# Windowed attention feeding a normalised MLP: score and value steps in pairs from one PSUM pool

## The chip, the cores and the metric

The kernel runs on one core of a Trainium2 chip. The metric is device time in microseconds (us); before the change the median of three runs is 309.67 us (309.27 to 309.78). The core's engines are TensorE (PE in the profile, with its weight loads as PEld), VectorE (DVE), ScalarE (ACT), GpSimd (POOL) and SyncE (SP, which here issues most DMAs). Each works through its own list of instructions in order and waits on semaphores for the others.

## The reference

Attention with a causal window of 64 positions, for 8 batches of 8 heads, 576 positions and a head width of 64. Its output, with the heads side by side, is the input of a normalised two-layer MLP with a residual:

```python
scores = scale * np.matmul(q, k.transpose(0, 1, 3, 2))          # scale = 1/8
mask = (rel >= 0) & (rel < 64)                                   # rel = query - key
attn = softmax(np.where(mask, scores, -1e9)); y = np.matmul(attn, v)
x = y.transpose(0, 2, 1, 3).reshape(8, 576, 512)
xn = (x - mean) / np.sqrt(var + 1e-06) * g_ln
out = x + np.maximum(xn @ w_ch1, 0.0) @ w_ch2                    # 512 -> 2048 -> 512
```

## The kernel before

**Groups.** The work is cut into nine groups. Groups 0 to 7 are the first 512 positions of the eight batches, four blocks of 128 queries each. Group 8 collects the last 64 positions of all batches; its blocks are called tails, and block i of it belongs to batches 2i and 2i+1.

**Attention of one block** has two parts on TensorE.

- A score step (`s_mm`): 16 matmuls, each 64 rows deep (one head's width), write 64 queries against 128 keys. Even heads go to one 2 KB PSUM tile and odd heads to another, both from the pool `ps_s`, which has two buffers. Two exponentials on ScalarE (L294), one a tile, write the probabilities `pt` in fp16, and `s_mask` (L301) multiplies them by the window's mask on VectorE.
- A value step (`b_step`): 16 matmuls (L321), each 64 columns wide, write the 128 by 8 by 65 values, with the row sums as the 65th column, into one 4 KB PSUM tile `xps` from the pool `ps_x`, which has one buffer. VectorE takes the reciprocal of the sums (L324), scales into `x_norm` (L327) and computes mean and variance (L329, L332).

From group 2 on `z_step` then makes the normalised row `z` on GpSimd in four instructions (L351 to L354), and `zt_step` transposes it into `zT` (by DMA, or for two blocks by TensorE).

**MLP of one group.** From group 2 on it has 30 units, numbered from 0. Units 0 to 15 are `l1`: four matmuls with 512 columns each (L401) into a tile of `ps_mm`, which has two buffers, and a ReLU out of it on ScalarE into `hrT` (L405). So unit i+2 can't begin before the ReLU of unit i has read its tile. Units 16 to 29 are `stage`: the second layer as seven half-size products, two units each, in the order 1, 2, 6, 5, 7, 4, 3. `product` (L478) sums into the PSUM banks A, B and C; product 6 goes on in bank A on top of product 1. `post` (L485) adds a bank to `x_norm` on VectorE, and product 6 can't begin before the `post` of product 1 has read bank A. Products 6, 5, 7 and 3 take sums of `hrT` that VectorE makes in `s_sums` (L452): for the first eight units in slots 8 to 11, for the next four in slots 13 and 14, for the last four in slots 15, 15, 19 and 21.

**The order is written by hand.** Each engine executes in the order in which the loop at the end issues. While group g runs its MLP, the attention of group b = g+1 is issued between its units, and the loads, casts and transposes of group n = g+2: `at(i, f, ...)` puts a call behind unit i, in slot i, and calls in one slot come in the order of the `at` lines. Before the change the steps of group b stand so:

```python
at((2, 7, 12)[j - 1], s_mm, b, j)          # j = 1, 2, 3; block 0 in slot 27 of the group before
at((3, 8, 13)[j - 1], s_mask, b, j)
at((2, 7, 12, 17)[j], b_step, b, j)
at((2, 7, 12, 17)[j], z_step, b, j)
```

Four casts of q and k to fp16 (L128) on GpSimd, two for each, stand in slots 11 (three) and 16 (one); the k casts are transposed by TensorE (`t_main`, L229), the q casts by DMA from SP's queue in slot 13. Group 1 has other units, with the same scheme. The last group's first layer uses half-size products too (L592), in tiles that it takes from all pools.

Of the kernel before, what the change touches and what calls it, by code (L numbers as in the profile page):

```python
# [20 lines left out]
def kernel(  # L21
# [34 lines left out]
    ps_s = ctx.enter_context(tc.tile_pool(name="pss", bufs=2, space=PSUM))  # L56
    ps_x = ctx.enter_context(tc.tile_pool(name="psx", bufs=1, space=PSUM))
# [9 lines left out]
    mhalf = p_const.tile([128, 1], FP32, tag="mhalf", name="mhalf")  # L67
# [192 lines left out]
    def s_mm(g, j, pe_mask=False):  # L260
        sc = [ps_s.tile([128, NHP, 2, 64], FP32, tag="sc", name=f"sc_{g}_{j}_{par}") for par in range(2)]
        pt = p_pt.tile([128, 2, NHP, 2, 64], FP16, tag="pt", name=f"pt_{g}_{j}")
        pts[(g, j)] = pt
        if pe_mask:
            m = mbias[:, :]
            mb = bass.AP(tensor=m.tensor, offset=m.offset, ap=[m.ap[0], [0, NHP * 2], m.ap[1]])
            for par in range(2):
                nc.tensor.matmul(
                    out=sc[par][:, :].rearrange("p h w i -> p (h w) i"), lhsT=ident16, rhs=mb,
                    start=True, stop=False, skip_group_check=True,  # L270
                )
        for hp in range(NHP):
            for iw in range(2):
                for par in range(2):
# [11 lines left out]
                    nc.tensor.matmul(out=sc[par][:, hp, iw, :], lhsT=lhsT, rhs=rhs,  # L286
                                     start=not pe_mask, stop=True, skip_group_check=pe_mask)

        for par in range(2):
            o, i = pt[:, par], sc[par][:, :]  # L290
            if XQ <= g < NGRP - 1:
                o = o.rearrange("p h w (r j) -> p (h w) r j", j=4)
                i = i.rearrange("p h w (j r) -> p (h w) r j", j=4)
            nc.scalar.activation(out=o, in_=i, func=AF.Exp, bias=0.0, scale=scale)  # L294
# [8 lines left out]
    def b_step(g, kb):  # L303
        kblk = f"{g}_{kb}"
        sfx, nb = ("r", 2) if g == NGRP - 1 else ("", None)
        if kb % 2 == 0:
            if (g, kb // 2) not in x_norm:
                for h in ((1, 0) if g // 2 == 2 else (0, 1)):
                    x_norm[(g, h)] = p_xn.tile([128, 2, DM], FP32, tag="xn" + sfx, name=f"xn_{g}_{h}", bufs=nb)
        xv = x_norm[(g, kb // 2)][:, kb % 2, :]  # L310
        xn = xv.rearrange("p (h d) -> p h d", h=H)
        xps = ps_x.tile([128, H, 128], FP32, tag="xps", name=f"xps_{kblk}")
        pt = pts.pop((g, kb))
        for h in range(H):
            par, hp = h % 2, h // 2
            for r in range(2):
                if sfx:
                    rhs = vT[kb][:, r, h, :]
                else:
                    rhs = (vA if r else vB)[g][:, kb, h, :]  # L320
                nc.tensor.matmul(out=xps[64 * r:64 * r + 64, h, :D + 1], lhsT=pt[:, par, hp, r, :], rhs=rhs,  # L321
                                 start=True, stop=True)
        rcp = p_blk.tile([128, H], FP32, tag="rcp", name=f"rcp_{kblk}")
        nc.vector.reciprocal(out=rcp, in_=xps[:, :, D])  # L324
        rcp_b = bass.AP(tensor=rcp.tensor, offset=rcp[:, :].offset,
                        ap=[rcp[:, :].ap[0], rcp[:, :].ap[1], [0, D]])
        nc.vector.tensor_tensor(out=xn, in0=xps[:, :, 0:D], in1=rcp_b, op=ALU.mult)  # L327
        stats = p_blk.tile([128, nc.vector.BN_STATS_DIM], FP32, tag="stats", name=f"stats_{kblk}")
        nc.vector.bn_stats(out=stats, in_=xv)  # L329
        if g not in mvg:  # L330
            mvg[g] = p_grp.tile([128, 4, 2], FP32, tag="mvg" + sfx, name=f"mvg_{g}", bufs=1 if sfx else 2)
        nc.vector.bn_aggr(out=mvg[g][:, kb, :], in_=stats)  # L332
        if g < 2 and (g, kb) != (0, 2):
            z_step(g, kb)

    def z_step(g, kb):
# [15 lines left out]
        nc.gpsimd.tensor_tensor(out=rs, in0=ve, in1=mhalf, op=ALU.pow)  # L352
# [39 lines left out]
    def mlp_units(g, split=0, three=False, seven=True):  # L392
# [173 lines left out]
        def l1_product(n, d):  # L566
# [11 lines left out]
            }[n]  # L578
            if n == 1:
                pool, tag = (ps_mm, "mm") if d == 2 else (ps_s, "sc")  # L580
# [451 lines left out]
```

## Time and profile before

| | |
|---|---|
| median of three runs | 309.67 us |
| the profiled execution, first to last instruction | 305.9 us |
| PE busy | 295.4 us (97%), 3061 matmuls |
| DVE busy | 220.6 us (72%), 412 instructions |
| POOL busy | 173.3 us (57%), 256 instructions |
| ACT busy | 150.7 us (49%), 253 instructions |
| PE's longest wait on another engine | 2.3 us, once, at the start |
| granted TensorE clock, mean | 0.995 |

The profile's span runs from the first to the last instruction of one execution; the 3.8 us up to the median lie around it. Idle time of an engine that is not the bottleneck costs nothing, so what counts is what holds PE up. In a timeline the columns are the start, the duration, the engine, the line, the operation, output and inputs, their shape and the count; a bracket at the end gives idle time ahead of the instruction and what ended it. Ends of matmuls are modelled, so PE is best read by its starts.

### The profile page before, as it was taken

How to read it: one execution, taken by the hardware profiler on the slowest of the kernel's cores; microseconds unless marked ns; L12 is line 12 of the kernel's file. 1: busy time of each engine (PE TensorE's matmuls, PEld its weight loads, DVE VectorE, ACT ScalarE, POOL GpSimd, SP SyncE). 2: the span in 40 equal slices, each digit the busy share in tenths (PEclk: the TensorE clock that was granted, in tenths of full speed). 3: DMA queues.
4: the chain of work that ended last, by engine and by line, in shares of the span. 5: the costliest groups of instructions: out<-in, count | busy, mean ns of one | idle time of the engine just before them, and what ended most of it. 6: DMA issues, size and time to landing. Idle time of an engine off the chain costs nothing.

```text
span 305.9 us, 7582 instructions
## 1 busy us (share of the span) xinstructions
PE 295.4 (97%) x3061; PEld 196.4 (64%) x3061; DVE 220.6 (72%) x412; ACT 150.7 (49%) x253; POOL 173.3 (57%) x256
## 2 busy tenths in 40 slices
PE   6989999999999999999999999999999999999992
PEld 4557545687454478547854786469646854788882
DVE  0778696767766995589656965896669685789972
ACT  2586635587227733775157527752475046306500
POOL 7589676564952789179806983698146507014300
PEclk9999999999999999999999999999999999999998
DMA  8999999999776997899189997993790399003014
GB/s 191 266 385 301 314 366 286 303 284 236 150 181 228 243 172 147 280 280 127 35 243 303 204 160 245 298 155 70 215 175 19 53 189 208 19 17 139 0 38 103
DMA packets 113669, 58.35 MB, mean 191 GB/s; under 512 B 83617, under 2 KB 104609, under 8 KB 113634
## 3 DMA queue, kind: packets, MB, share of 16 engines
q1 hardware_dynamic: 112576, 54.67, 74.0%
q0 software_dynamic: 768, 2.80, 3.8%
q8 instruction: 24, 0.39, 0.5%
q10 hardware_dynamic: 290, 0.40, 0.5%
q14 instruction: 11, 0.09, 0.1%
HBM read 38.80 MB, written 9.44 MB: 158 GB/s over the span
## 4 chain that ended last, share of the span: by engine, by line
PE 89%; SPq 4%; DMA 2%; POOL 1%; ACT 1%; DVE 1%; issue 0%; ACTq 0%
PE hps L401 30%; PE pA L478 12%; PE pB L478 8%; PE pC L478 8%; PE hph L537 6%; PE ch L413 6%; PE xps L321 4%; PE sc L286 4%; PE ch L554 3%; PE tp L229 3%; PE lA L592 2%; DMA w1s<-in_moe_w_ch_dram 2%; SPq L141 2%; POOL w1g L190 1%; SPq L89 1%; PE lC L592 1%
## 5 line engine op out<-in xcount | busy, mean ns | idle before, releaser
L401 PE MATMUL hps<-zT,w1g 128*128 128x512 f16 x416 | 95.3, 380 | 0.0
L405 ACT ACTIVATE hrT<-hps 128x512 f16<-128x512 f32 x104 | 62.3, 599 | 39.3 <-PE hps L401 35.7
L401 PEld LDWEIGHTS <-w1g 128*128 128x128 f16 x416 | 38.6, 98 | 43.3 <-issue 0.7
L294 ACT ACTIVATE pt<-sc 128x512 f16<-128x512 f32 x72 | 39.0, 594 | 27.7 <-PE sc L286 20.5
L478 PEld LDWEIGHTS <-sS 128*128 128x128 f16 x448 | 43.4, 98 | 4.9
L351 POOL TENSOR_SCALAR rsz<-mvg 128x1 f32<-128x1 f32 x28 | 10.2, 364 | 60.6 <-DVE mvg L332 59.8
L128 POOL CAST qk<-qk 128x1024 f16<-128x1024 f32 x32 | 36.3, 1147 | 11.3 <-DMA qk<-in_k_dram 5.6
L478 PEld LDWEIGHTS <-hrT 128*128 128x128 f16 x336 | 32.4, 98 | 5.5 <-ACT hrT L637 0.3
L301 DVE TENSOR_TENSOR pt<-pt,mask 128x1024 f16<-128x1024 f16 x32 | 27.5, 867 | 8.4 <-ACT pt L294 8.4
L215 ACT COPY qkT<-tp 128x1024 f16<-128x1024 f16 x16 | 16.1, 1012 | 34.1 <-PE tp L229 34.1
L485 DVE TENSOR_TENSOR xn<-pA,xn 128x512 f32<-128x512 f32 x28 | 19.2, 685 | 16.7 <-PE pA L478 11.1
L478 PE MATMUL pC<-w2s,sS 128*128 128x256 f16 x224 | 27.1, 273 | 0.0
L478 PE MATMUL pA<-wT,sS 128*128 128x256 f16 x224 | 26.9, 273 | 0.0
L354 POOL TENSOR_SCALAR z<-xn,rsz 128x512 f16<-128x512 f32 x28 | 24.9, 888 | 2.9
L327 DVE TENSOR_TENSOR xn<-xps,rcp 128x512 f32<-128x512 f32 x36 | 24.9, 691 | 1.5 <-DMA out_dram<-xn 0.3
L329 DVE BATCH_NORM_STATS2 stats<-xn 128x6 f32<-128x512 f32 x36 | 25.0, 695 | 1.2
L324 DVE RECIPROCAL rcp<-xps 128x8 f32<-128x8 f32 x36 | 7.3, 204 | 24.7 <-PE xps L321 24.7
L452 DVE TENSOR_TENSOR sS<-hrT 128x512 f16<-128x512 f16 (+1 forms) x40 | 24.5, 613 | 0.6 <-ACT hrT L405 0.6
L537 PE MATMUL hph<-zT,w1g 128*128 128x256 f16 x192 | 23.8, 273 | 1.0 <-DVE zT L371 0.5
L321 PEld LDWEIGHTS <-pt 128*64 128x64 f16 x576 | 12.2, 110 | 13.7 <-issue 5.5
L352 POOL TENSOR_TENSOR rsz<-rsz,mhalf 128x1 f32<-128x1 f32 x28 | 19.4, 692 | 2.3
L147 POOL CAST vA<-v 128x1024 f16<-128x1024 f32 (+2 forms) x19 | 17.4, 930 | 5.6 <-DMA v<-in_v_dram 5.6
(113 smaller groups left out, 448.9 us busy)
## 6 DMA issues: line engine op xcount, KB each, us to landing
out_dram<-xn SPq DMA_DIRECT2D x33, 256.0 KB, 2.8
qk<-in_q_dram SPq DMA_DIRECT2D x16, 512.0 KB, 6.2
qk<-in_k_dram SPq DMA_DIRECT2D x16, 512.0 KB, 6.9
v<-in_v_dram SPq DMA_DIRECT2D x32, 256.0 KB, 7.7
w2s<-in_moe_w_ch_dram SPq DMA_DIRECT2D x9, 512.0 KB, 9.2
w1s<-in_moe_w_ch_dram SPq DMA_DIRECT2D x4, 512.0 KB, 7.3
tk<-in_k_dram SPq DMA_DIRECT2D x8, 256.0 KB, 4.5
tv<-in_v_dram SPq DMA_DIRECT2D x8, 256.0 KB, 5.0
```

What stands on the lines that cost most here:

```text
L128: nc.gpsimd.tensor_copy(out=dst[:, :].rearrange("p (a j) e d -> p a e j d", j=j), in_=t[:, :].rearrange("p (a e j d) -> p a e j d", e=2, j ...
L294: nc.scalar.activation(out=o, in_=i, func=AF.Exp, bias=0.0, scale=scale)
L301: nc.vector.tensor_tensor(out=ptv, in0=ptv, in1=mb, op=ALU.mult)
L321: nc.tensor.matmul(out=xps[64 * r:64 * r + 64, h, :D + 1], lhsT=pt[:, par, hp, r, :], rhs=rhs, start=True, stop=True)
L327: nc.vector.tensor_tensor(out=xn, in0=xps[:, :, 0:D], in1=rcp_b, op=ALU.mult)
L329: nc.vector.bn_stats(out=stats, in_=xv)
L354: nc.gpsimd.tensor_scalar(out=z, in0=xv, scalar1=rs, scalar2=nm, op0=ALU.mult, op1=ALU.add)
L401: nc.tensor.matmul(out=hps, lhsT=w1g[:, kc, 128 * hc:128 * (hc + 1)], rhs=zT[g][:, kc, :], start=(kc == 0), stop=(kc == NKC - 1),)
L405: nc.scalar.activation(out=hrT[:, hc, :], in_=hps, func=AF.Relu, bias=0.0, scale=1.0)
L452: nc.vector.tensor_tensor(out=o, in0=x, in1=y, op=op)
L478: nc.tensor.matmul(out=o, lhsT=a[:, c, 128 * p:128 * p + 128], rhs=wv[:, c, :], start=(first and (p == 0 or split_c) and c == 0), stop=(c ...
L537: nc.tensor.matmul(out=hps[:, e], lhsT=w1g[:, kc, 128 * hc:128 * (hc + 1)], rhs=zT[g][:, kc, 256 * half:256 * half + 256], start=(kc == 0) ...
```

## The change

One PSUM pool, `ps_a`, with two buffers of 4 KB takes the place of `ps_s` and `ps_x`. A score step now writes both head parities into one 4 KB tile and has one exponential over 1024 columns. `s_mm` is split into `s_pe` (the matmuls) and `s_exp` (the exponential). In groups 2 to 6 blocks 0 and 1 of group b have their score steps behind each other in slot 26 of the group before (slot 28 in group 1) and their value steps behind each other in slot 2; blocks 2 and 3 have their score matmuls in slot 7 and their value steps in slot 13, with the exponential of block 2 in slot 7 and that of block 3 in slot 10. `b_step` takes several blocks: first all matmuls, then reciprocal and scaling of each, then the statistics of each. `z_pair` makes two blocks' `z` with a shared start. All four q and k casts stand in slot 11. The tails of groups 3 and 5 move from slots 1, 2, 5 and 11 to 18, 19, 22 and 27. The last group's tiles come out of `ps_a` too.

```diff
-    ps_s = ctx.enter_context(tc.tile_pool(name="pss", bufs=2, space=PSUM))
-    ps_x = ctx.enter_context(tc.tile_pool(name="psx", bufs=1, space=PSUM))
+    ps_a = ctx.enter_context(tc.tile_pool(name="psa", bufs=2, space=PSUM))
...
-    def s_mm(g, j, pe_mask=False):
-        sc = [ps_s.tile([128, NHP, 2, 64], FP32, tag="sc", name=f"sc_{g}_{j}_{par}") for par in range(2)]
+    scs = {}
+
+    def s_pe(g, j, pe_mask=False):
+        sc = ps_a.tile([128, 2, NHP, 2, 64], FP32, tag="att", name=f"sc_{g}_{j}")
+        scs[(g, j)] = sc
...
-                    nc.tensor.matmul(out=sc[par][:, hp, iw, :], lhsT=lhsT, rhs=rhs,
+                    nc.tensor.matmul(out=sc[:, par, hp, iw, :], lhsT=lhsT, rhs=rhs,
                                      start=not pe_mask, stop=True, skip_group_check=pe_mask)
 
-        for par in range(2):
-            o, i = pt[:, par], sc[par][:, :]
...
-            nc.scalar.activation(out=o, in_=i, func=AF.Exp, bias=0.0, scale=scale)
+    def s_exp(g, j):
+        sc = scs.pop((g, j))
+        pt = p_pt.tile([128, 2, NHP, 2, 64], FP16, tag="pt", name=f"pt_{g}_{j}")
+        pts[(g, j)] = pt
+        o, i = pt[:, :], sc[:, :]
...
+        nc.scalar.activation(out=o, in_=i, func=AF.Exp, bias=0.0, scale=scale)
+
+    def s_mm(g, j, pe_mask=False):
+        s_pe(g, j, pe_mask)
+        s_exp(g, j)
...
-    def b_step(g, kb):
+    def b_step(g, *kbs):
...
+        for kb in kbs:
...
+            xps = ps_a.tile([128, H, 128], FP32, tag="att", name=f"xps_{g}_{kb}")
...
+        for kb in kbs:
+            xn = x_norm[(g, kb // 2)][:, kb % 2, :].rearrange("p (h d) -> p h d", h=H)
+            rcp = p_blk.tile([128, H], FP32, tag="rcp", name=f"rcp_{g}_{kb}")
+            nc.vector.reciprocal(out=rcp, in_=xpss[kb][:, :, D])
...
+            nc.vector.tensor_tensor(out=xn, in0=xpss[kb][:, :, 0:D], in1=rcp_b, op=ALU.mult)
+        for kb in kbs:
+            stats = p_blk.tile([128, nc.vector.BN_STATS_DIM], FP32, tag="stats", name=f"stats_{g}_{kb}")
+            nc.vector.bn_stats(out=stats, in_=x_norm[(g, kb // 2)][:, kb % 2, :])
+            nc.vector.bn_aggr(out=mvg[g][:, kb, :], in_=stats)
...
+    def z_pair(g, kb0):
+        t = p_blk.tile([128, 3, 2], FP32, tag="rs2", name=f"rs2_{g}_{kb0}", bufs=2)
+        var = mvg[g][:, kb0:kb0 + 2, 1]
+        nc.gpsimd.tensor_scalar(out=t[:, 0, :], in0=var, scalar1=1.0, scalar2=EPS, op0=ALU.mult, op1=ALU.add)
+        nc.gpsimd.tensor_tensor(out=t[:, 1, :], in0=t[:, 0, :], in1=mhalf, op=ALU.pow)
+        for e in range(2):
...
+            nc.gpsimd.tensor_scalar(out=nm, in0=mvg[g][:, kb, 0:1], scalar1=rs, scalar2=-1.0,
+                                    op0=ALU.mult, op1=ALU.mult)
+            nc.gpsimd.tensor_scalar(out=z, in0=x_norm[(g, kb // 2)][:, kb % 2, :], scalar1=rs, scalar2=nm,
+                                    op0=ALU.mult, op1=ALU.add)
...
+            if not lbank:
+                lbank["X"] = ps_a.tile([128, 2, 2, 256], FP32, tag="att", name="lX")
+                lbank["Y"] = ps_a.tile([128, 2, 2, 256], FP32, tag="att", name="lY")
...
-            at(31, s_mm, 3, 0)
-            at(31, s_mask, 3, 0)
-            for i, (x, half) in zip((12, 24, 12, 28), ((0, 0), (1, 0), (0, 1), (1, 1))):
+            at(28, s_mm, 3, 0)
+            at(28, s_mm, 3, 1)
+            at(29, s_mask, 3, 0)
+            at(30, s_mask, 3, 1)
+            for i, (x, half) in zip((12, 22, 12, 25), ((0, 0), (1, 0), (0, 1), (1, 1))):
...
+        n = g + 2
+        if g > 1 and n < B:
+            at(11, alloc_qkT, n)
+            at(11, cast_qk, n, 0, (0,))
+            at(11, cast_qk, n, 1, (0,))
+            at(11, cast_qk, n, 0, (1,))
+            at(11, cast_qk, n, 1, (1,))
         if g > 1 and b < B:
+            at(2, b_step, b, 0, 1)
+            at(2, z_pair, b, 0)
+            at(7, s_mm, b, 2)
+            at(7, s_pe, b, 3)
+            at(8, s_mask, b, 2)
+            at(10, s_exp, b, 3)
+            at(11, s_mask, b, 3)
+            at(13, b_step, b, 2, 3)
+            at(13, z_pair, b, 2)
             for j in range(4):
-                if j:
-                    at((2, 7, 12)[j - 1], s_mm, b, j)
-                    at((3, 8, 13)[j - 1], s_mask, b, j)
-                at((2, 7, 12, 17)[j], b_step, b, j)
-                at((2, 7, 12, 17)[j], z_step, b, j)
-                at((12, 12, 18, {3: 24, 5: 23}.get(b, 22))[j], zt_step, b, j)
+                at((12, 12, 22, {3: 24, 5: 23}.get(b, 22))[j], zt_step, b, j)
-        for n, i in enumerate(TAILS.get(g, ())):
-            ts = (13, 13, 17, 22) if n else (1, 2, 5, 11)
+        for m, i in enumerate(TAILS.get(g, ())):
+            ts = (18, 19, 22, 27) if b < B else (13, 14, 17, 22) if m else (1, 2, 5, 11)
...
-            at(16, cast_qk, n, 1, (1,) if n >= XQ else (0, 1))
...
-            for i, (x, half) in zip((13, 18, 13, 22) if g == 2 else (13, 17, 13, 21),
-                                    ((0, 0), (1, 0), (0, 1), (1, 1))):
+            for i, (x, half) in zip((13, 17, 13, 21), ((0, 0), (1, 0), (0, 1), (1, 1))):
                 at(i, t_main, n, x, half, 0)
-            at(27, s_mm, n, 0)
-            at(28, s_mask, n, 0)
+            at(26, s_mm, n, 0)
+            at(26, s_mm, n, 1)
+            at(27, s_mask, n, 0)
+            at(28, s_mask, n, 1)
```

## The prediction

> **What bounds the kernel now.** I read the page first, then PE's waits, then timelines of groups 4 and 7.
>
> ```profile
> PE 295.4 (97%) x3061; PEld 196.4 (64%) x3061; DVE 220.6 (72%) x412; ACT 150.7 (49%) x253; POOL 173.3 (57%) x256
> PE 89%; SPq 4%; DMA 2%; POOL 1%; ACT 1%; DVE 1%; issue 0%; ACTq 0%
> ```
>
> PE is the bound: 97% busy and 89% of the chain that ended last. The waits view has five entries for PE, together 4.2 us. So the change counts by what it takes from PE's stream or puts into it. Both can be read at group 4's slot 12, where value step 2 is followed by score step 3:
>
> ```profile
> 167.86 0.38 PE L401 MATMUL hps<-zT,w1g 128*128 128x512 f16 x1
> 168.17 0.22 PE L321 MATMUL xps<-vB,pt 128*64 128x65 f16 x1
> ...
> 168.42 0.19 PE L321 MATMUL xps<-vB,pt 128*64 128x65 f16 x1
> 168.43 0.20 PE L321 MATMUL xps<-vA,pt 128*64 128x65 f16 x1
> 168.55 0.41 PE L286 MATMUL sc<-qkT,qkT 64*128 64x64 f16 x16
> 168.89 0.39 PE L401 MATMUL hps<-zT,w1g 128*128 128x512 f16 x1
> ```
>
> Read the starts. Matmuls of 512 columns follow each other at 0.216 us, but 167.86 to 168.17 is 0.31: entering a step with another tile shape costs 0.093. Inside a value step two matmuls start every 0.032, but 168.43 to 168.55 is 0.12: going from value to score shape costs 0.098. Leaving to 512-column matmuls costs the same (0.096) and 0.010 more at the next matmul. A value step takes 0.38, a score step 0.34, each with its leaving edge.
>
> The covers are read in two more places. ScalarE's ReLU between units:
>
> ```profile
> 161.41 0.60 ACT L405 ACTIVATE hrT<-hps 128x512 f16<-128x512 f32 x1 [0.27 <-PE hps L401]
> 162.27 0.60 ACT L405 ACTIVATE hrT<-hps 128x512 f16<-128x512 f32 x1 [0.27 <-PE hps L401]
> ...
> 248.79 0.60 ACT L405 ACTIVATE hrT<-hps 128x512 f16<-128x512 f32 x1 [0.22 <-PE hps L401]
> 249.28 1.08 ACT L294 ACTIVATE pt<-sc 128x512 f16<-128x512 f32 x2
> 250.24 1.32 ACT L405 ACTIVATE hrT<-hps 128x512 f16<-128x512 f32 x2
> 250.90 0.31 PEld L401 LDWEIGHTS <-w1g 128*128 128x128 f16 x2 [0.26 <-issue]
> ```
>
> The unit read at 161.41 ended at 161.21; its ReLU ends at 162.01, and the unit that reuses its tile starts at 162.07. That margin of 0.06 is all there is, although ScalarE is only 49% busy. In group 7 a lone tail score step puts two exponentials ahead of a ReLU. That ReLU ends at 250.85, and PE, due at 250.76, starts at 250.90: 0.14 lost.
>
> VectorE between slot 12 and product 6 of group 4 (last line: product 6 on PE):
>
> ```profile
> 168.66 0.21 DVE L324 RECIPROCAL rcp<-xps 128x8 f32<-128x8 f32 x1 [0.16 <-PE xps L321]
> 168.91 0.69 DVE L327 TENSOR_TENSOR xn<-xps,rcp 128x512 f32<-128x512 f32 x1
> 169.63 0.69 DVE L329 BATCH_NORM_STATS2 stats<-xn 128x6 f32<-128x512 f32 x1
> 170.46 1.46 DVE L301 TENSOR_TENSOR pt<-pt,mask 128x1024 f16<-128x1024 f16 x1
> 171.84 1.25 DVE L452 TENSOR_TENSOR sS<-hrT 128x512 f16<-128x512 f16 x1
> 173.12 0.42 DVE L452 TENSOR_TENSOR sS<-sS,hrT 128x512 f16<-128x512 f16 x1
> ...
> 174.93 0.68 DVE L485 TENSOR_TENSOR xn<-pA,xn 128x512 f32<-128x512 f32 x1
> ...
> 175.92 0.49 PE L478 MATMUL pA<-wT,sS 128*128 128x256 f16 x3
> ```
>
> VectorE works without a break here. The addition out of bank A ends at 175.61 and product 6, which must wait for it, starts at 175.92: 0.31 to spare (the same in groups 2, 3 and 5; 1.04 in group 6). The mask took 1.46 against a median of 0.69, and the next sum 1.25 against 0.42, while GpSimd ran the three casts of slot 11 (169.35 to 172.82): about 0.8 more each.
>
> **The change part by part.**
>
> *Edges saved.* In the instruction order PE enters a step from other matmuls 55 times before and 50 after, leaves as often, and goes directly between value and score shape 17 times before and 2 after. That saves 5 x 0.093 + 5 x 0.107 + 15 x 0.098 = 2.47 us. The 20 new joins between two steps of one kind have no row: between 0 (as between heads inside a step) and 0.098 each. I take 0, since the shape doesn't change; the other end is 1.96.
>
> *One exponential for two.* Two of 512 columns take 1.08. One of 1024: L294's 0.594, plus 0.437 for 512 more columns (L215's copy of 1024 columns, 1.012, less L369's of 512, 0.575) = 1.03. It frees 36 x 0.05 us on ScalarE, which is hidden except where PE waited for an exponential (0.7 us in the prologue, the two places of group 7): I take -0.2 in all.
>
> *`z_pair`* takes 20 small instructions off GpSimd (L351 and L352, 10 each). No one on the path waits for it: 0; if the z rows came late, the transposes in slots 22 to 24 would, and block 3's `z` is made 4 slots earlier than before. Moves of tails, k transposes and `zt_step` leave counts alone: 0, between -0.3 and +0.3. On SP's queue the two tails' `z` transposes move from slot 11 to 27, behind block transposes and ahead of stores that nothing on the path reads: 0. The q transposes stay in slot 13; group 4's landed at 183.56, 0.12 before the score step at 183.68 that reads them. One slot earlier that step would wait up to 1 us, but not once the waits below have delayed it by more.
>
> *The exponential of slot 10.* Score steps 2 and 3 stand in slot 7, where PE's pair (0.59) gives ScalarE time for the first exponential. The second comes in slot 10 between two ReLUs, with no attention on PE there. Counted from the end of unit 10: ReLU 10 starts at 0.21, the exponential at 0.71 (ReLUs overlap what follows by 0.1), ReLU 11 at 1.65 instead of 1.07, and ends at 2.25. Unit 13, due at 1.73, starts at 2.30: 0.57 lost, in each of groups 2 to 6: +2.85. The ends: 0 if something held PE anyway, 0.7 from group 7's row (0.14, plus the 0.34 + 0.20 that its score step took on PE).
>
> *The value pair of slot 13 and product 6.* Before, VectorE had block 2's value work and a mask ahead of the sums; now it has two blocks' value work, and PE has less to do until product 6. From the first value matmul, PE needs: pair 0.67, units 14 and 15 1.74, product 1 1.75, k transposes 0.45, product 2 1.75 = 6.35. VectorE: first reciprocal at 0.49 (168.17 to 168.66), twice 0.97 for reciprocal and scaling, twice 0.83 for statistics, six sums 2.26 (173.12 to 174.93 for five, and 0.45), addition 0.68 and 0.06 for the signal = 7.09. Product 6 waits 0.74 in groups 2 and 4. In groups 3 and 5 the tail's score step of slot 18 gives PE 0.44 more: 0.30. In group 6, without k transposes: 1.19. Sum 3.27.
>
> *Four casts in a row.* GpSimd is through `z_pair` of slot 2 at about 10.9 us of the group (value work on VectorE until 6.9, six instructions of 2.4 + 1.1, some delay) and casts until about 15. Now the third sum of slot 10, the mask of block 3 (ready after its exponential, 12.75) and the fourth sum fall among the casts. The first is absorbed by VectorE's wait for the exponential. Mask and fourth sum cost 0.8 each by the rows above, less the 0.65 that VectorE would have had before the pair (14.06 against 14.71): 1.0 more in groups 3, 4 and 5; in group 2, where four w2 sums slow `z_pair` down and the casts start later, 0.7. Sum 3.7; ends 0 (casts miss the sums) and 2.0 a group (all four meet one, 8.0).
>
> The Trainium skill's "SBUF — State Buffer", section "Who interferes with whom", speaks against this part of the change: VectorE instructions with two SBUF inputs and GpSimd instructions that read SBUF hold a shared port in turn, and the later one waits for the whole earlier one. That agrees with the stretched rows, and by it a collision would cost up to a whole cast, 1.03 instead of 0.8, and the sum above would be about 5.3 instead of 3.7.
>
> *Sum*: -2.47 - 0.2 + 2.85 + 3.27 + 3.7 = +7.15. The profiled execution of 305.9 becomes 313.05; with the 3.8 us around it, the median of 309.67 becomes 316.8.
>
> **The rivals.**
>
> *R1, faster: no wait appears.* Only the savings stay: 307.0. The place is ScalarE's ReLU and VectorE's chain; it decides if ReLUs may come 0.57 later and the chain is 0.74 shorter than its rows. For it: average shares of 49% and 72%. Against it: group 7's 0.14 and the 0.31 before product 6.
>
> *R2, the exponential alone.* VectorE is in time, as it needs 6.35 instead of 7.09 (were sums or statistics to overlap more than shown). -2.67 + 2.85: 309.9.
>
> *R3, both waits, but no collision.* The casts fall between VectorE's fp16 work: -2.67 + 6.12 = +3.45: 313.1. For it: GpSimd's time after `z_pair` is the least certain of my readings, and 4 sums already ran undisturbed in slots 8 to 11.
>
> *R4, all casts collide.* Block 3's mask then comes after 15.2 us, late for the pair's second step too: 8.0 instead of 3.7 and more, 321.
>
> The granted clock is 1.00 through group 4 and 0.995 on the mean, and the waits above are of 0.3 to 2.2 us. The Trainium skill's "TensorE: Matmul & The Clock Gate", section "Part 1: The HAM clock gate (the "warmup" mystery)", has the clock halved after about 3.4 us without work; no run here shows that.
>
> **How the numbers follow.** Forecast 0.50, R3 0.26, R4 0.10, R2 0.06, R1 0.06, anything else 0.02. The predicted time is the forecast's, 316.8; its own range, with 0.5 to 1.4 a group for the casts, is 314.8 to 318.4. The range leaves out R1, R2 and two thirds of R4, about 2 in 10: 311.0 to 320.5. A measurement of this kernel tells about 0.2% (0.6 us) from no change. Faster by more: R1 and a little of R2, 0.07. Within: 0.03. Slower: the rest, 0.90.
>
> **What the profile after would show.** Edges: two value steps of together 0.67 us, with starts 0.03 apart across the join. The exponential: L297 with about 1.03 us, and in each of five groups one hps matmul some 0.57 late, after the second exponential. Product 6: PE idle before its first matmul in groups 2 to 6, released by the addition out of bank A, most in group 6 without casts. Casts: masks of 1.4 us in slot 11, and a reciprocal of slot 13 that starts later than 0.49 after its first matmul. I am wrong if product 6 starts straight after product 2, or if no gap stands ahead of unit 13.

## The result and the profile after

The changed kernel takes 321.42 us (median of four runs, 319.92 to 322.97) against 309.73 before: ratio 1.035 (95% interval 1.028 to 1.042). The forecast was 316.8 with a range of 311.0 to 320.5. The direction was right, the size too small by 4.6 us, and the time lies just outside the range. All run times here and below are medians without the few executions more than 1.5% above the fastest of the same kernel; each ratio is to the kernel before as measured beside it, whose medians lie between 308.7 and 309.7 us.

The page of the changed kernel, the lines that answer to those of before (busy time by engine, and the chain that ended last):

```profile
PE 297.4 (93%) x3061; PEld 196.5 (61%) x3061; DVE 226.8 (71%) x412; ACT 148.3 (46%) x217; POOL 161.0 (50%) x236
PE 71%; DVE 15%; ACT 4%; SPq 4%; DMA 2%; POOL 1%; issue 1%; ACTq 0%
```

PE's share of the chain fell from 89% to 71%, and VectorE's rose from 1% to 15%: PE now waits for it. PE's waits of the changed kernel (releaser, us in total, times, longest):

```profile
PE xps L327 <- DVE pt L308: 6.1, 5, 1.8
...
PE hps L425 <- ACT hrT L429: 1.8, 5, 0.4
...
PE pA L502 <- DVE xn L509: 1.3, 2, 0.7
...
PE lX L617 <- DVE hrT L632: 0.8, 1, 0.8
...
PE lX L617 <- ACT hrT L662: 0.7, 1, 0.7
...
PE lX L617 <- ACT u2sums L629: 0.5, 2, 0.3
```

The first entry is the largest: value matmuls that wait for a mask. Three of its five waits, 5.3 us together, lie behind the start of group 2. Here is the place in group 3, in the timeline of the changed kernel:

```profile
135.84 1.14 DVE L308 TENSOR_TENSOR pt<-pt,mask 128x1024 f16<-128x1024 f16 x1 [2.83 <-ACT pt L297]
136.38 0.31 POOL L207 MEMSET qkT<- 128x256 f16 x1
136.64 5.56 POOL L127 CAST qk<-qk 128x1024 f16<-128x1024 f32 x4
136.90 1.52 DVE L476 TENSOR_TENSOR sS<-hrT 128x1024 f16<-128x1024 f16 x1
138.45 1.41 DVE L476 TENSOR_TENSOR sS<-sS,hrT 128x1024 f16<-128x1024 f16 x1
139.62 1.02 PE L425 MATMUL hps<-zT,w1g 128*128 128x512 f16 x4 [0.36 <-ACT hrT L429]
139.78 1.52 DVE L476 TENSOR_TENSOR sS<-hrT 128x1024 f16<-128x1024 f16 x1
...
140.82 0.19 PE L327 MATMUL xps<-vA,pt 128*64 128x65 f16 x1
141.22 1.52 DVE L308 TENSOR_TENSOR pt<-pt,mask 128x1024 f16<-128x1024 f16 x1
142.67 0.68 DVE L476 TENSOR_TENSOR sS<-hrT,sS 128x1024 f16<-128x1024 f16 x1
142.80 0.22 PE L327 MATMUL xps<-vB,pt 128*64 128x65 f16 x1 [1.78 <-DVE pt L308]
```

The casts run on GpSimd from 136.64 to 142.20, and VectorE's fp16 work that starts beside them takes 1.41 to 1.52 where the first sum after them takes 0.68. Block 3's mask ends at 142.74, so PE, through with block 2's value matmuls, starts block 3's at 142.80, 1.98 after the matmul at 140.82 and not 0.03. It is the same in groups 4 (1.96) and 5 (1.98). The line at 139.62 shows unit 13 late behind its ReLU.

Three pairs of windows in the changed kernel, with the granted clock (columns: window; its length; busy us of PE, PEld, DVE, ACT, POOL, each with its instructions; PEclk; DMA share; GB/s):

```profile
139.80:143.21 3.41, 1.63 (x37) 0.90 (x36) 3.41 (x4) 0.85 (x2) 2.40 (x2) 1.00 0.76 151
143.21:146.62 3.41, 3.41 (x12) 1.21 (x10) 3.27 (x10) 0.60 (x1) 0.00 (x0) 0.50 0.75 144
...
173.93:177.34 3.41, 1.65 (x22) 0.62 (x19) 3.41 (x3) 1.65 (x4) 3.19 (x3) 1.00 0.98 170
177.34:180.75 3.41, 3.04 (x22) 1.40 (x23) 3.31 (x9) 0.53 (x1) 0.00 (x0) 0.50 1.02 219
208.06:211.47 3.41, 2.11 (x24) 0.82 (x22) 3.41 (x3) 2.11 (x4) 3.41 (x3) 1.00 1.04 199
211.47:214.88 3.41, 2.56 (x29) 1.53 (x30) 3.34 (x7) 0.84 (x2) 0.25 (x1) 1.00 1.23 149
```

Behind the waits of groups 3 and 4 the clock is halved for 3.41 us: units 14 and 15 take 0.427 us a matmul, not 0.216. Behind that of group 5 it is not. Before the change the clock was never halved between 9.6 and 303 us.

One more place, in the last group, timeline of the changed kernel:

```profile
291.06 0.60 PE L617 MATMUL lX<-zsums,w1S 128*128 128x256 f16 x4
...
291.69 0.69 DVE L632 TENSOR_TENSOR hrT<-lX,zsums 128x512 f16<-128x512 f32 x1
...
292.44 0.60 PE L617 MATMUL lX<-zsums,w1S 128*128 128x256 f16 x4 [0.78 <-DVE hrT L632]
```

The matmuls at 291.06 write one half of the 4 KB tile `lX`, those at 292.44 the other. They wait until VectorE has read the first half.

The span grew by 14.5 us (305.9 to 320.4). Intervals between the first matmuls of the groups, from PE's starts, in the profiles of all kernels (us; "first layer" is the last group's, from the start of its first matmul to that of its last; e and f are the experiments below):

| | up to group 2 | 2 | 3 | 4 | 5 | 6 | 7 | first layer |
|---|---|---|---|---|---|---|---|---|
| before | 92.50 | 31.37 | 31.30 | 31.35 | 31.30 | 29.04 | 26.44 | 16.00 |
| after | 94.38 | 32.03 | 34.93 | 34.59 | 33.47 | 29.66 | 26.32 | 18.46 |
| e1_last | 95.01 | 32.01 | 34.90 | 34.76 | 33.44 | 29.65 | 26.32 | 16.00 |
| e2_act_casts | 93.65 | 32.61 | 31.72 | 32.95 | 31.72 | 29.65 | 26.31 | 18.46 |
| e3_score_split | 93.07 | 32.01 | 34.83 | 33.84 | 33.45 | 29.50 | 26.32 | 18.46 |
| e4_stats_late | 95.08 | 32.39 | 33.22 | 34.85 | 33.23 | 28.76 | 27.73 | 18.46 |
| f1_fill | 93.56 | 32.02 | 33.46 | 33.86 | 33.46 | 29.66 | 26.32 | 18.46 |
| f2_unpaired | 93.75 | 31.38 | 31.28 | 31.37 | 31.27 | 29.03 | 26.32 | 18.45 |
| f4_fourth | 94.33 | 34.21 | 33.48 | 34.25 | 33.48 | 29.66 | 26.32 | 18.47 |
| f3_best | 92.70 | 31.18 | 31.56 | 31.91 | 31.57 | 28.71 | 26.33 | 16.00 |
| f5_best_nosplit | 94.34 | 31.34 | 31.57 | 31.90 | 31.56 | 28.87 | 26.32 | 16.00 |
| f6_best_q1 | 95.42 | 31.51 | 31.12 | 31.97 | 31.12 | 28.71 | 26.32 | 16.01 |
| f7_best_27 | 93.87 | 31.58 | 31.12 | 31.58 | 31.12 | 28.71 | 26.32 | 16.01 |

From there to the last matmul it is 10.69 in every row. From group 2 on the stages repeat to within 0.05 us wherever the code is the same and the clock is up. Up to group 2 they scatter by 2.9 us. So the experiments are read by stage first, which means in one profiled execution each, and by their times where these can tell.

### The profile page after: what moved, and what is told of

Same layout as the page of the kernel before. It is cut to its first block, busy times and chain, and to the rows that moved or that the text cites. A ratio compares the mean times of both kernels' runs of the same rounds, so it can differ in the third digit from the quotient of the medians.

```text
span 320.4 us, 7527 instructions
## 1 busy us (share of the span) xinstructions
PE 297.4 (93%) x3061; PEld 196.5 (61%) x3061; DVE 226.8 (71%) x412; ACT 148.3 (46%) x217; POOL 161.0 (50%) x236
## 4 chain that ended last, share of the span: by engine, by line
PE 71%; DVE 15%; ACT 4%; SPq 4%; DMA 2%; POOL 1%; issue 1%; ACTq 0%
PE hps L425 22%; PE pA L502 11%; PE pC L502 8%; PE pB L502 7%; PE ch L437 5%; DVE sS L476 5%; PE hph L561 5%; DVE pt L308 3%; PE xps L327 3%; PE ch L578 2%; DMA w1s<-in_moe_w_ch_dram 2%; PE tp L228 2%; ACT pt L297 2%; PE sc L286 2%; SPq L140 2%; PE lX L617 2%
## 5 line engine op out<-in xcount | busy, mean ns | idle before, releaser
L425 PE MATMUL hps<-zT,w1g 128*128 128x512 f16 x416 | 98.4, 387 | 1.8 <-ACT hrT L429 1.8
L429 ACT ACTIVATE hrT<-hps 128x512 f16<-128x512 f32 x104 | 61.6, 599 | 60.4 <-PE hps L425 56.3
L425 PEld LDWEIGHTS <-w1g 128*128 128x128 f16 x416 | 39.7, 99 | 48.7 <-issue 7.8
L297 ACT ACTIVATE pt<-sc 128x1024 f16<-128x1024 f32 x36 | 36.2, 1020 | 23.8 <-PE sc L286 23.6
L127 POOL CAST qk<-qk 128x1024 f16<-128x1024 f32 x32 | 38.5, 1224 | 13.7 <-DMA qk<-in_q_dram 7.2
L308 DVE TENSOR_TENSOR pt<-pt,mask 128x1024 f16<-128x1024 f16 x32 | 29.0, 918 | 19.1 <-ACT pt L297 19.0
L348 POOL TENSOR_SCALAR rs<-mvg 128x2 f32<-128x2 f32 x10 | 2.6, 264 | 69.0 <-DVE mvg L341 69.0
L476 DVE TENSOR_TENSOR sS<-hrT 128x512 f16<-128x512 f16 (+1 forms) x40 | 27.4, 685 | 1.3 <-ACT hrT L429 1.2
L327 PEld LDWEIGHTS <-pt 128*64 128x64 f16 x576 | 11.7, 111 | 16.1 <-DVE pt L308 7.4
L146 POOL CAST vA<-v 128x1024 f16<-128x1024 f32 (+2 forms) x19 | 18.5, 991 | 5.3 <-DMA v<-in_v_dram 5.3
L561 PEld LDWEIGHTS <-w1g 128*128 128x128 f16 x192 | 17.7, 98 | 4.7 <-POOL w1g L189 1.6
L327 PE MATMUL xps<-vB,pt 128*64 128x65 f16 x256 | 13.2, 198 | 6.9 <-DVE pt L308 6.1
```

The costliest lines, as they stand in the source:

```text
L127: nc.gpsimd.tensor_copy(out=dst[:, :].rearrange("p (a j) e d -> p a e j d", j=j), in_=t[:, :].rearrange("p (a e j d) -> p a e j d", e=2, j ...
L308: nc.vector.tensor_tensor(out=ptv, in0=ptv, in1=mb, op=ALU.mult)
L425: nc.tensor.matmul(out=hps, lhsT=w1g[:, kc, 128 * hc:128 * (hc + 1)], rhs=zT[g][:, kc, :], start=(kc == 0), stop=(kc == NKC - 1),)
L429: nc.scalar.activation(out=hrT[:, hc, :], in_=hps, func=AF.Relu, bias=0.0, scale=1.0)
L476: nc.vector.tensor_tensor(out=o, in0=x, in1=y, op=op)
L561: nc.tensor.matmul(out=hps[:, e], lhsT=w1g[:, kc, 128 * hc:128 * (hc + 1)], rhs=zT[g][:, kc, 256 * half:256 * half + 256], start=(kc == 0) ...
```

## The experiments

My theory after the two traces: the loss is (a) the mask that comes late beside the casts, and with it (b) the halved clock, (c) unit 13 behind the exponential, (d) product 6 behind VectorE, and (e) the last group's shared tiles. The rival in each case: VectorE or ScalarE is late for another reason, and the repair changes nothing. All but one of the experiments start from the changed kernel.

**The last group's tiles.**

```diff
-                lbank["X"] = ps_a.tile([128, 2, 2, 256], FP32, tag="att", name="lX")
-                lbank["Y"] = ps_a.tile([128, 2, 2, 256], FP32, tag="att", name="lY")
...
-                    ... if d == 2 else lbank["X"][:, d % 3]
+                    ... if d in (1, 2) else \
+                    ps_a.tile([128, 2, 2, 256], FP32, tag="att", name=f"lA_{d}")[:, 0]
...
-                    lbank["Y"][:, d // 2]
+                    ps_a.tile([128, 2, 2, 256], FP32, tag="att", name=f"lC_{d}")[:, 0]
```

> The changed kernel, with a PSUM tile of its own for each of the last group's first-layer accumulations (A of quarters 1 and 2 from the pool of the MLP tiles, A of 0 and 3 and C of 0 and 2 each a fresh 4 KB tile), in place of halves of two shared 4 KB tiles. Theory (the halves are tracked as one tile, so a product into one half waits for ScalarE's or VectorE's read of the other): PE's first-layer products of the last group take 13.4 us as before the change, not 15.9, and the time falls by 2.4 us against the changed kernel, to about 319.0. Rival (the 2.45 us come from VectorE and ScalarE being later in that group, whatever the tiles): the products stay at 15 us or more and the time within 0.5 us of 321.4.

Measured: 319.7 us, ratio to before 1.030 (1.021 to 1.038). The first layer takes 16.00, as before the change, against 18.46 (the expectation's 13.4 and 15.9 differ by about as much), and all other stages from group 2 on stay within 0.2 of the changed kernel's. So (e) is shown, 2.46 us, and its cause is the sharing of a tile.

**The casts on ScalarE.**

```diff
-            at(11, cast_qk, n, 0, (0,))          # four on GpSimd
...
+            at(16, cast_qk, n, 0, (0,), nc.scalar.copy)
+            at(16, cast_qk, n, 1, (0,), nc.scalar.copy)
+            at(17, cast_qk, n, 0, (1,), nc.scalar.copy)
+            at(17, cast_qk, n, 1, (1,), nc.scalar.copy)
...
-            for i, (x, half) in zip((13, 17, 13, 21), ...
+            for i, (x, half) in zip((17, 21, 17, 23), ...
```

> The changed kernel, with the four q and k casts of groups 2 to 5 taken off GpSimd: ScalarE does them in slots 16 and 17, behind the last ReLU; the DMA transposes of q follow in slot 17, the k transposes in slots 21 and 23. Theory (GpSimd's casts slow VectorE's fp16 work down, block 3's mask comes late, PE waits about 2 us at the value pair of groups 3, 4 and 5, and its clock is then halved): the mask of slot 11 takes 0.7 us, the three waits of 2 us (5.9 us in all) go, and so does the halved clock behind them (2.9 us). Product 6 loses the k transposes of slot 17 as cover and VectorE's delay no longer hides behind PE's: its waits grow by about 0.45 in group 2, 0.7 in groups 3 and 5 and 1.1 in group 4, less what it has now, some +2.7 in all. Sum -6.1: 315.3. Rival (block 3's mask is late because its exponential stands in slot 10 and the sums stand ahead of it, casts or no casts): PE keeps waits of 1.5 us or more at the value pair, and the time stays at 321 or rises.

Measured: 316.74 us, ratio 1.024 (1.016 to 1.032). The value pairs of groups 3 to 5 take 0.64 us, the clock stays at 1.00 to the end, and groups 3 and 5 fall to 31.72. VectorE in group 3 from block 2's mask to block 3's, without the casts:

```profile
135.69 1.11 DVE L308 TENSOR_TENSOR pt<-pt,mask 128x1024 f16<-128x1024 f16 x1 [2.84 <-ACT pt L297]
136.73 0.68 DVE L476 TENSOR_TENSOR sS<-hrT 128x1024 f16<-128x1024 f16 x1
...
138.96 0.69 DVE L308 TENSOR_TENSOR pt<-pt,mask 128x1024 f16<-128x1024 f16 x1 [0.22 <-ACT pt L297]
```

Three sums and block 3's mask take 0.68 to 0.69 now, and that mask ends 13.4 us after the group's start and not 16.3. Block 2's mask is stretched as before (1.11 and 1.14), so not by the casts; in both traces GpSimd is making `z` then. PE's waits show what takes over:

```profile
PE pA L502 <- DVE xn L509: 2.7, 5, 0.7
```

Product 6 now waits in all five groups. From group 2 to the last matmul the kernel takes 214.11 us against 220.14, so the saving there is 6.0 and near the 6.1 expected; that the medians differ by 4.7 only is within the scatter ahead of group 2. Group 4 stays 1.2 above groups 3 and 5: product 6 waits 0.9 there, and a PE transpose of k another 0.7 behind ScalarE's copy into `zT`. The theory holds for (a) and (b): without the casts beside it, VectorE is in time for the value pair.

**Block 3's score matmuls with their exponential.**

```diff
-            at(7, s_pe, b, 3)
...
-            at(10, s_exp, b, 3)
+            at(10, s_mm, b, 3)
```

> The changed kernel, with the score matmuls of block 3 moved from slot 7 to slot 10, just ahead of their exponential (as every other score step stands); slot 7 keeps block 2 alone. Theory (the exponential of slot 10 delays the ReLU of unit 11 and so unit 13 by 0.52 us, since PE has no attention work there): with 0.3 us of score matmuls and their two edges on PE there, unit 13 is no longer late; -0.52 + 0.2 for the pair's two extra edges = -0.3 in each of five groups, -1.6 in all: 319.8. Rival (ScalarE is behind by the exponential wherever PE's score matmuls stand): unit 13 is still 0.5 late after them and the extra edges come on top, +1.0: 322.4.

Measured: 321.02 us, ratio 1.037 (1.029 to 1.044). The wait on the ReLU has left PE's list altogether, as the theory has it. But groups 2 and 5 are as long as they were (32.01 and 33.45 against 32.03 and 33.47), and group 6 is only 0.16 shorter (29.50 against 29.66). The other waits are longer (the third wait of product 6 is group 4's, see below):

```profile
PE xps L327 <- DVE pt L308: 6.3, 4, 1.9
...
PE pA L502 <- DVE xn L509: 1.9, 3, 0.7
```

Both expectations fail. PE starts the value pair only 0.15 earlier (14.01 instead of 14.16 us after the group's start): of the 0.52, about 0.2 go into the edges of the step split off, and two delays of 0.07, too short for the list, stay between the units. In groups 2 and 5 even the 0.15 is hardly seen, since VectorE is no earlier: counted from the group's start, product 6 of group 2 begins at 21.26 us (21.28 in the changed kernel), and block 3's mask releases PE in group 5 at 16.37 (16.39). So moving the score matmuls gains 0.15 a group at most, and next to nothing where a wait on VectorE follows. Group 4 is shorter by 0.75, because its clock stayed up this time.

**Statistics behind the sums.**

```diff
-            at(13, b_step, b, 2, 3)
-            at(13, z_pair, b, 2)
+            at(13, lambda: b_step(b, 2, 3, stat=False))
+            at(17, b_stats, b, 2, 3)
+            at(17, z_pair, b, 2)
```

> The changed kernel, with the statistics of blocks 2 and 3 and their shared start of z moved from slot 13 to slot 17, behind the sums of slots 13 to 15 and the addition out of bank A on VectorE. Theory (product 6 waits for VectorE, which has two blocks' statistics, 1.7 us, ahead of the sums): the waits of product 6 in groups 2, 5 and 6 (0.7, 0.2 and 0.9) go; in groups 3 and 4, where PE itself is late, nothing changes: -1.8, to 319.6. Rival (the wait is set by product 1's own end and the addition, 0.75 us, whatever stands ahead): product 6 keeps its 0.7 and 0.9, time 321.4. If z of blocks 2 and 3 now comes too late for the transposes of slots 22 to 24, a new wait stands at the start of the next group.

Measured: 322.57 us, ratio 1.042 (1.034 to 1.050), so no faster. The waits of product 6 do go: group 6 falls by 0.90 and group 5 by 0.24, which shows (d). (Group 3 is 1.7 shorter because its clock stayed up this time.) But `z` of blocks 2 and 3 comes too late. In group 2 a PE transpose of `z` and one of a tail wait, about 1.0 in all. In group 7 a score step waits for a tail's k, whose DMA transpose SP issues 10.9 us after the group's start and not 8.5; that the `z` transposes ahead of it in SP's queue hold it up is argued, not tested:

```profile
PE sc L286 <- DMA tkT<-tk: 1.4, 1, 1.4
```

**Dummy matmuls in the gap.** Eight matmuls are added ahead of the value pair in groups 3 to 5; nothing is taken away.

```diff
+    def fill(m):
+        o = ps_t.tile([128, 512], FP32, tag="t0", name="fill")
+        for _ in range(m):
+            nc.tensor.matmul(out=o, lhsT=ident16, rhs=w2s[:, 0, :], start=True, stop=True)
...
+            if g in (3, 4, 5):
+                at(13, fill, 8)
             at(13, b_step, b, 2, 3)
```

> The changed kernel, with eight matmuls of 512 columns (1.73 us at the full clock, on data that is there, into a PSUM bank that nobody uses then) ahead of the value pair of blocks 2 and 3 in groups 3, 4 and 5, where PE waits about 2 us for block 3's mask. They add to the work and take no wait away. Theory (the clock is halved because PE does too little in one of the 3.41 us intervals in which it is granted): the granted clock stays at 1.00 to the last stores, the units behind the pair run at 0.216 us a matmul, and the time falls although PE does more, by up to the 2.9 us that the halved clock cost in the profile, to 318.5 to 319.5. Rival (the halved clock has another cause, or costs nothing because VectorE sets the pace there anyway): the time stays at 321.4 or rises.

The windows at the same three places, in this kernel:

```profile
140.83:144.24 3.41, 3.37 (x46) 1.72 (x44) 3.34 (x7) 0.60 (x1) 0.54 (x1) 1.00 0.84 162
174.96:178.38 3.42, 3.38 (x49) 2.20 (x49) 3.32 (x8) 1.20 (x2) 0.00 (x0) 1.00 1.23 222
209.10:212.51 3.41, 3.37 (x45) 2.15 (x38) 3.31 (x9) 1.20 (x2) 0.00 (x0) 1.00 1.12 88
```

PE is busy throughout, and the clock stays at 1.00 to the end of the work. Group 3 falls from 34.93 to 33.46 and group 4 from 34.59 to 33.86, 2.2 us for more work; group 5, where the clock had not been halved, is the same (33.46 and 33.47). Group 4 gains less because product 6 waits 0.7 there again, which the halved clock had hidden. The median, 320.9 us (ratio 1.038, 1.033 to 1.044), can't show 2 us against the scatter ahead of group 2. By stage (b) is shown, with 2.2 us in the profiled execution.

**The old slots with the new pool.** The changed kernel's pool, score and value steps and last group, with the loop, and so the slots, of the kernel before.

> The pool of two 4 KB tiles, the single exponential and the last group's shared tiles of the changed kernel, with the slots of the kernel before (score steps in slots 27, 2, 7 and 12, value steps in 2, 7, 12 and 17, three casts in slot 11 and one in 16, tails in 1, 2, 5 and 11). Theory (the new slots carry all losses but the last group's): no wait of PE on a mask or on a first-layer ReLU, clock 1.00, the last group's 2.46 us remain and the single exponential gives 0.2, so 2.3 us above the kernel before (1.007 of it). Rival (the shared pool itself makes score and value steps wait for each other's readers): 4 us or more above it.

Measured: 311.59 us, ratio 1.009 (1.006 to 1.012), which holds the theory's 1.007 and not the rival's 1.013. Groups 2 to 6 take what they took before, to 0.03, and the first layer 18.45. So from group 2 on all loss but the last group's comes from the slots; the pool and the single exponential cost nothing there.

**The fourth cast back in slot 16.**

```diff
-            at(11, cast_qk, n, 1, (1,))
+            at(16, cast_qk, n, 1, (1,))
```

> The changed kernel, with the last of the four casts back in slot 16, where it stood before the change; three stay in slot 11. Theory (each cast on GpSimd that meets an fp16 sum or a mask lengthens it by about 0.8 to 1.1 us, and the last one meets the fourth sum or block 3's mask): the wait at the value pair of groups 3 to 5 falls from 2.0 us to 0.9 to 1.2, about -3 in all, and with gaps that short the clock stays up, -2.9: 315.5 to 318.5. Rival (mask and sums are late because of their number in slots 8 to 11 and not because of how many casts run beside them): the wait stays at 1.8 us or more and the time at 321.

Measured: 322.5 us, ratio 1.044 (1.039 to 1.048). At the value pair the theory is right: the wait falls from 1.98 to 1.12 by starts, mask 3 takes 0.68 again, and the clock stays up. But the gain is lost at once, as the waits show:

```profile
PE tp L228 <- POOL qk L127: 4.4, 4, 2.0
PE xps L327 <- DVE pt L308: 3.3, 4, 0.9
```

In slot 16 the cast stands behind `z_pair` of slot 13 on GpSimd, whose first instruction waits for two blocks' statistics, and the k transposes of slot 21 wait for the cast, up to 2.0 us. Neither theory nor rival had this. With the value steps in slot 13, the fourth cast is in the way in slot 11 and late in slot 16.

**All repairs together.** The last group's tiles and block 3's score matmuls as above; the two k casts on ScalarE in slot 16, with transposes in slots 18 and 19; block 3's statistics and `z` alone in slot 17.

```diff
-            at(11, cast_qk, n, 0, (1,))
-            at(11, cast_qk, n, 1, (1,))
+            at(16, cast_qk, n, 0, (1,), nc.scalar.copy)
+            at(16, cast_qk, n, 1, (1,), nc.scalar.copy)
...
-            at(13, z_pair, b, 2)
+            at(13, b_stats, b, 2)
+            at(13, z_step, b, 2)
+            at(17, b_stats, b, 3)
+            at(17, z_step, b, 3)
```

> The changed kernel with four repairs: the last group's accumulations in tiles of their own; the two k casts of groups 2 to 5 on ScalarE in slot 16 (their transposes in slots 18 and 19, the q casts stay on GpSimd in slot 11); the score matmuls of block 3 in slot 10 ahead of their exponential; the statistics and z of block 3 in slot 17, behind the sums. Theory (the losses are what the traces show, and VectorE, freed of two collisions and one block's statistics, is no longer late): -2.46 for the last group, -5.9 for the waits on masks, -2.9 for the clock, -1.8 for product 6 and -0.3 a group for unit 13: 14.6 less than 321.4, 306.9, and so below the kernel before. Rival (VectorE stays the pace-maker of slots 8 to 20, so that each repair turns into a wait elsewhere, as when block 3's score matmuls alone were moved): 311 or more.

Measured: 309.15 us, ratio 1.0035 (1.0000 to 1.0071). Nearly all of the loss is gone, but the version is not below the kernel before: it lies between the theory's 306.9 and the rival's 311. From group 2 on it takes 207.95 against 207.50 to the last matmul. Two waits are left there. In groups 3 to 5 the value pair still waits for block 3's mask, 0.4 us by starts; in the list these are three of four, and the longest lies ahead of group 2:

```profile
PE xps L327 <- DVE pt L308: 1.3, 4, 0.5
```

In group 4 the score pair of slot 26 also takes 0.86 instead of 0.57.

**The same without moving the score matmuls** (block 3's in slot 7 again):

> The version with four repairs, less one of them: the score matmuls of block 3 stand in slot 7 again, as in the changed kernel, with their exponential alone in slot 10. Theory (the exponential of slot 10 costs 0.52 us of PE at unit 13 in every group, and shows in the time wherever PE does not wait for VectorE right after it): in groups 2 and 6, where the repaired version has no wait on a mask, 0.52 less two edges of 0.2, +0.3 each; in groups 3 to 5 the delay takes the place of the 0.3 to 0.5 us that PE waited for the mask, 0. Sum +0.6 against the repaired version, 309.8. Rival (the forecast's reading, 0.5 a group whatever else happens): +1.5 and over, 310.7.

Measured: 311.17 us, ratio 1.006 (1.003 to 1.009). By the time alone that is the rival's (310.7 and over). By stage, groups 3 to 5 stay (31.57, 31.90, 31.56), groups 2 and 6 grow by 0.16 each. So (c) counts only where no wait on VectorE follows, as the theory has it, with half the size. The median lies 2.0 above the version it is compared with (the kernel before, measured beside each, differs by 0.4), far more than the stages from group 2 on (0.3). In the two profiles 1.6 of it falls ahead of group 2, where the two are the same code.

**One cast less beside VectorE**, the second q cast on ScalarE too, and then **the score pair in slot 27** and the second k transposes in slot 21:

```diff
-            at(11, cast_qk, n, 1, (0,))
+            at(16, cast_qk, n, 1, (0,), nc.scalar.copy)
```

> The version with four repairs, and the second q cast on ScalarE too (slot 16, its DMA transpose in slot 17; k transposes in slots 19 and 20), so that one cast a group is left on GpSimd in slot 11. Theory (the 0.3 to 0.5 us that PE still waits for block 3's mask in groups 3 to 5 come from the second cast meeting a sum): these waits go, 1.0 to 1.3 us in all, 308.0 against a kernel before of 308.7 to 309.2. Rival (ScalarE's three casts make the k transposes or the q transposes late for product 6 or for the score pair of slot 26): new waits of 0.3 us or more a group there, 309 to 310.

```diff
-            at(26, s_mm, n, 0)
-            at(26, s_mm, n, 1)
+            at(27, s_mm, n, 0)
+            at(27, s_mm, n, 1)
```

> The version with one cast a group left on GpSimd, with the score pair of blocks 0 and 1 one slot later (27 instead of 26) in groups 2 to 5 and the second k transposes in slot 21. In the profile of that version the score pair of slot 26 waited 0.3 us in group 2 and 0.5 us in group 4 for q's DMA transposes, and product 6 lost 0.4 us in group 4 at the k transposes of slot 20. Theory (what is left of the losses is these three waits): they go, 1.2 us in all, and the version ends about 1 us below the kernel before: 308.0, ratio 0.996 to 0.998. Rival (the masks, a slot later, are now late for the value pair of the next group's slot 2, or other waits of this size come up): no change, ratio 0.999 to 1.002.

Measured: 309.17 us, ratio 0.9992 (0.9962 to 1.0023), and 309.16 us, ratio 0.9998 (0.9973 to 1.0023), so the rival's in both. In the first, groups 3 and 5 fall to 31.12, free of waits, and groups 2 and 4 have the waits of slot 26 (group 4 another 0.4 at k transposes). In the second these go, and group 4 falls by 0.4, but group 2 doesn't: in both groups a tail's k transposes now wait nearly 0.4 us for ScalarE. From group 2 on this last version takes 0.4 us less than the kernel before, which its time can't show. No version beats the kernel before measurably.

## Why the prediction was too low

The direction was right, and so were two of the waits (unit 13 and product 6). The steps that failed are the casts' term, which had too few collisions and the wrong place for their cost, and two terms that the sum didn't have: the halved clock and the last group's tiles. Product 6 was over-sized and hides part of this. From group 2 on the changed kernel takes 12.65 us longer in the profiles (220.14 against 207.50), 5.5 more than the sum of +7.15.

*Edges: right.* Score pairs take 0.57 us and value pairs 0.64, where 0.585 and 0.67 were forecast with joins at 0; the starts across the join are 0.03 apart. Groups 3 and 5 of the last version, which have no wait left (and one pair less), are 0.18 shorter than before.

*Exponential: right.* 1.02 us against 1.03.

*`z_pair`, tails, transposes: right*, 0 in groups 2 to 7 of the changed kernel.

*The exponential of slot 10: right in place and size.* Unit 13 is 0.52 late in each of five groups (forecast 0.57), 2.6 in all. What it would be worth to repair is another matter: the one repair tried gained 0.15 of the 0.52, and in groups 3 to 5 the wait for the mask takes up that.

*Product 6: over-sized.* The forecast had 0.74, 0.30, 0.74, 0.30 and 1.19, sum 3.27; measured are about 0.69, 0, 0, 0.22 and 0.89, sum 1.8. In groups 3 to 5 PE is late itself, after the mask, and VectorE has caught up.

*The casts: the step that failed, in place and size.* That casts stretch VectorE's fp16 work was right. But the forecast let them run from 10.9 us of the group, meet three instructions, the first of them at no cost, and only shorten VectorE's time before the value pair and so delay product 6: 1.0 us a group, sum 3.7. In group 3 they start at 10.2 (136.64 - 126.41) and cost four instructions time: three sums (+0.84, +0.73, +0.84) and mask 3 (+0.84), 3.25 us. So mask 3 is late itself. It comes after block 2's value matmuls are through, and PE stands still between the two value steps, in three groups for 1.95 each, 5.8 us. Taking the casts away removed these waits. In group 2 there is none, against 0.7 forecast; there the casts start 3 us later and meet only the fourth sum. The forecast's R4 had such a wait ("late for the pair's second step too"), with a chance of 0.10. That R4's 321 us comes near the measured time is luck: it kept 3.27 for product 6 and had neither clock nor last group. The Trainium skill's "SBUF — State Buffer", section "Who interferes with whom", would have each collision cost up to a whole cast; here a sum lost 0.73 to 0.84 us beside casts of 1.39 (four in 5.56), where one alone takes 1.04.

*The clock: left out.* The forecast saw waits of 0.3 to 2.2 us and took the clock at 1.00. A gap of 2 us was enough in groups 3 and 4, and cost 2.2 us.

*The last group: left out.* The diff showed `lX` and `lY`, and the forecast had no term for them: 2.46 us.

*Against which time.* The forecast put 3.8 us between the span and the time. All runs with both have 1.7 to 2.0. So the profiled execution of before would be a run of about 307.7, 2.0 faster than the median, and that of the changed kernel, 322.17, is 0.75 slower than its own: 14.5 - 2.0 - 0.75 = 11.7, the measured difference. Against that the sum of +7.15 was 4.5 short.

The ledger from group 2 on, as the waits stand in the trace (not what repairing each alone would give back): -2.67 for edges and exponential as forecast, +2.6 for unit 13, +5.8 for the masks, +1.8 for product 6, +2.2 for the clock, +2.46 for the last group, sum 12.2. The trace has 12.65, so 0.5 stays open. Another 1.9 lies ahead of group 2, where the profiles scatter by 2.9.

## What to carry to other kernels

When an instruction is moved, lay it on the other engines' timeline of the slot it moves to, and count everything that it can meet there: four casts slowed four fp16 instructions, not two, and the wait came from the last of these. A delay ahead of a wait on a busy engine gives little back when it is repaired (0.15 us of PE here, and none of it in groups 3 to 5), until that engine is earlier. And two halves of one PSUM tile, written and read at different times, cost as much here (2.46 us) as the forecast had for all the shape changes that the pairing saves (2.47).

## What was not expected of the hardware

**The clock's intervals.** The borders at which the granted clock changes lie on a grid of 3.41 us in each trace: 143.21 and 177.34 are ten of them apart. Cut along that grid, the intervals tell the halving apart by PE's busy time. In the four traces with a drop, the interval just ahead of each of the six drops has 1.63 and 1.65 (changed kernel), 1.66 and 1.41 (last group's tiles), 1.49 (score matmuls moved) and 1.40 us (statistics moved) out of 3.41. In all thirteen traces no other interval between the tenth microsecond and the last matmuls has less than 1.84, and none of those was followed by a drop; among them is the same 2 us gap where a border cuts it in two. One interval of each kind, each with the one behind it, from the kernel with the score matmuls moved:

```profile
138.10:141.51 3.41, 1.49 (x25) 0.69 (x25) 3.41 (x4) 1.19 (x2) 2.75 (x2) 1.00 0.67 143
141.51:144.92 3.41, 3.41 (x23) 1.46 (x24) 3.31 (x8) 0.60 (x1) 0.00 (x0) 0.50 0.84 163
206.36:209.78 3.42, 1.84 (x23) 0.74 (x21) 3.42 (x3) 1.58 (x3) 3.16 (x3) 1.00 0.98 185
209.78:213.19 3.41, 3.08 (x33) 2.00 (x34) 3.31 (x9) 1.19 (x2) 0.00 (x0) 1.00 1.11 121
```

The Trainium skill's "TensorE: Matmul & The Clock Gate", section "Part 1: The HAM clock gate (the "warmup" mystery)", has such free-running intervals, of 3413 ns, which agrees; it has the clock fall after an idle one, where here an interval with PE busy for somewhat under half (1.40 to 1.66 of 3.41 us) was enough. So the same gap costs nothing in one trace and 0.7 to 1.7 us in another, depending on where a border of the grid falls: group 4's clock was halved in the changed kernel and not with the score matmuls moved, group 3's not with the statistics moved.

**Group 1.** From its first matmul to group 2's takes 36.07 us in the profile of before and 36.4 to 38.8 in the twelve others. The kernel with the old slots has 37.56 too, so the new slots aren't needed for it. The waits differ from trace to trace (`z` of VectorE, a DMA into `vB`, a mask). What makes them come and go was not tried and stays open.
